# Sliding-window attention and a mixture of experts on one core: attention's loads and stores moved, zeros' products added, the experts' stage in another order

## The chip, the cores and the metric

One NeuronCore of a Trainium2 chip runs the whole program in one launch. The metric is the device time in microseconds of that core; less is better. Its engines are TensorE (matrix products; PE in the profile, PEld its weight loads), VectorE (DVE), ScalarE (ACT), GpSimd (POOL) and SyncE (SP, which here only issues DMAs). Each engine works through its own queue of instructions in the order in which the program has them; they wait for each other by semaphores.

## The reference, cut to what matters

```python
def _attn_ref(q, k, v, n_sink, window):          # q, k, v: 4 x 8 x 768 x 64
    scores = scale * np.matmul(q, k.transpose(0, 1, 3, 2))
    keep = is_sink | in_window                   # 4 sinks, window of 128
    scores = np.where(keep, scores, -1000000000.0)
    a = np.exp(scores - max); a = a / (sum + 1e-09)
    return np.matmul(a, v)

def _moe_ref(x, w_gate, w1, w2):                 # x: 3072 x 512, 8 experts
    logits = x @ w_gate; cap = N // E
    order = np.argsort(-logits.flatten())        # best (token, expert) pairs first,
    ...                                          # an expert takes at most cap = 384 tokens
    for e in range(E):
        h = np.maximum(x[mask] @ w1[e], 0.0)     # 512 -> 1024
        out[mask] = h @ w2[e]                    # 1024 -> 512
```

## The kernel before, in words

**Attention** (`attention`, line 16) works on 24 blocks of 128 queries, numbered c: four batches of six. A block has products of queries and keys (`QK0`, `QK1`), masking and maxima on VectorE (`cp`, `mx`, `nm`), exponentials on ScalarE (`e0` to `e3`), transposes (`T`), copies (`pe0`, `pe1`), GpSimd's masking of the two diagonals (`A`, `B`), products with the values (`AV0`, `AV1`), a product that brings in the sinks (`XS`) and one that turns the result over (`X`), the division by the sums (`xe`) and the logits (`lm`). The block's rows are then stored to `x_dram` in DRAM (`xo`, line 162). Its queries, keys and values are loaded by `ldq`, `ldk` and `ldV` (lines 35 to 37). All of this is one list written out by hand, `SEQ` (line 199): a letter stands for an operation (`KINDS` gives which), and its n-th appearance for the n-th block. Every engine's queue is that list with the other engines' work left out, and so is SP's, which issues the loads and stores. The function `plan` (line 200) hands out buffers in the list's order: five for queries, five for values, six for the rows to be stored. Keys have one buffer a batch. A load has one more dependence, given by `paced` (line 25): it waits for the last activation that stands before it in the list, so that loads are spread over time. A store has none; it waits for its rows.

```python
def paced(d):
    if last: tc.add_manual_dep(d.ins,last[0].ins.name,...,reason="loads spread in time")
```

**The routing** finds for one expert after the other (in an order that the data set) the 384 tokens that it takes. `phase` (line 433) does it in six rounds; each is a compare on VectorE, a count on TensorE (`cnt`, `gather`, line 388), two or four short operations on VectorE, a product that sums over partitions (`dp`, line 483) and a maximum. Then come ranks (`pp`), the tokens' numbers (`ip`, `idx`) and the number of the expert (`ei`). Names are R0 to R7, so R1.dp3 is the sum of the fourth round for the second expert taken.

**An expert** k takes 384 tokens. GpSimd gathers their rows from `x_dram` in three DMAs (`G`, line 572), TensorE turns them over (`X`k.c.t: column block c, gather t; line 580), ScalarE and VectorE split them into a high and a low part (`xh`, `xl`). The weights come in eight chunks of 512 KB (`L`k.j, line 563) through two raw buffers; ScalarE takes the high part (`wh`, line 565), VectorE the low part (`wl`, `W`k.j, line 567), and only then is the raw buffer free for the chunk after the next. `M`k.f.c are the products with the first matrix (line 596; for the first two f of expert 0 lines 593 and 601, where the three products of high and low parts are taken apart), `hh` and `hl` the parts of the hidden values (lines 603 and 604), `N`k.t.f the products with the second (line 612), `y` and `S` the result and its scatter (lines 615 and 617). The order of all this on every engine is made by a list scheduler, `Graph.order` (line 263): it goes by the costs given with each operation, by a table of delays between engines (`ML`, line 238), by a number for each class of operations (`BIAS`, line 647) and by a look-ahead (`WIN`, line 646). The kernel then emits the instructions in that order, engine by engine.

**Zeros' products.** At named places (`FILL`, line 645) `warm` (line 429) puts products on TensorE whose result nobody reads: 128x384 of a matrix of ones, line 431.

Of the kernel before, what the change touches and what calls it, by code (L numbers as in the profile page):

```python
# [9 lines left out]
B,H,S,D=4,8,768,64  # L10
# [158 lines left out]
def layouts(q,k,v,wg,n_sink=4):  # L169
# [24 lines left out]
    P=(3,{'e0 e1 e2 e3':['T','hi','lo','nr']}),nmx=(4,{'nm0 nm1':['e0','e1','e2','e3']}),Z=(4,{'e0 e1 e2 e3':['ra']}),sx=(3,{'hi':['TS']}),  # L194
    PT=(3,{'pe0 pe1':['AV0','AV1']}),pS=(3,{'pS':['XS']}),E=(3,{'A0 A1':['AV0','AV1']}),v=(5,{'ldV':['AV0','AV1','AV0+','AV1+']}),
    r=(4,{'ra':['xe']}),at=(3,{'ae':['X']}),xt=(6,{'xe':['xo','lm']}))
DVEC=()
KINDS={'a': 'QK0', 'b': 'QK1', 'c': 'cp0', 'd': 'mx0', 'e': 'nm0', 'f': 'ldq', 'g': 'e0', 'h': 'fill', 'i': 'cp1', 'j': 'mx1', 'k': 'nm1', 'l': 'e1', 'm': 'e2', 'n': 'e3', 'o': 'U', 'p': 'Uc', 'q': 'um', 'r': 'gs', 's': 'ldk', 't': 'ldV', 'u': 'T', 'v': 'pe0', 'w': 'gl', 'x': 'pe1', 'y': 'nr', 'z': 'hi', 'A': 'A0', 'B': 'A1', 'C': 'lo', 'D': 'TS', 'E': 'pS', 'F': 'B0', 'G': 'AV0', 'H': 'B1', 'I': 'AV1', 'J': 'gc', 'K': 'vh', 'L': 'ae', 'M': 'vr', 'N': 'XS', 'O': 'ra', 'P': 'r', 'Q': 'lds', 'R': 'X', 'S': 'xe', 'T': 'lm', 'U': 'xo', 'V': 'fi', 'W': 'pr0', 'X': 'pr2', 'Y': 'pr1', 'Z': 'pr3', '0': 'pr5', '1': 'pr12', '2': 'pr15', '3': 'pr14', '4': 'pr4', '5': 'pr8', '6': 'pr6', '7': 'pr7', '8': 'pr13', '9': 'pr9', '!': 'pr11', '#': 'pr16', '$': 'pr10'}
SEQ='a b c d e f g h5 b a i j k l c d e m n h4 o p q r s t t i j k u g l h2 a v w m n s f x c d e y l f g b i h1 a j k z z m b n A B h1 u x c C h2 D C d E F h1 G H I y s e i J j k v m K L u l M h2 N g O P Q n R S a c v u B x f D y A E b d e s t O O v x T H P P F g i j B A z l G C I H L a c N F D E k n J t d R S G y s I e O m y L b g l u v a N z i x j k K C f D E z A c m R n O B F G d P e l S H I L g b i u A C D P f j t E a F c k d s B x v t m H G I L N R e n b s u S f g N R i l a s v x t b j k m S n c y d z C O D E B e z C l s P g u v x A i F y O G j M k H B I L A T z n a c H F d D E A U f e y F m N R S G I L b u t f C D g l a E O i T j P v k G x c d e B y N R U H I U t t T T m n S L s B b i l g u x T s z C D A F E y j k v a c d e n H G I a m u z L b g l c y A B f U F O d v N x e C D i E l g f O j k P P P R S s G H I b L t A N F J K B R m z C i n D E j k O S u n m G v U U f T T T H I L a x u x v N R c d b t a z e g S i j P s k l C D E t T c d N f y e n m B A F H G I L R S b A i y j O U u s k g l O U v f x n a N z C D R E m P c P d B F e y l G H I S L b O u U U i t z C s A g v D F E x j y k a z B C n O m c d e H G I b M L i u j y N f R P t l k s g a v x z S m B n b c d e N D f E g U A V F i j k R l C S f G H I s L a c d e b m n D i u z E V B H A F j t P s x B k H v A l G I f a g u t L F n N m v O c x y P R y S f d e N R S C D E b i J T z t l f G z u A B g j V V I s k C a x v O O L P K U N F n D c E P m d e H l t z T B M R S G I t A L b u a g i C v x y H V N j s k m D E n t R c d F G e I A S b g u L y y C D l i B x H a v b j k T T F E c d G B I O O n m e l z i j k T A U z y g U L t u x P C a F v m N D O E T C c T d T V e R G n g S H I l A W X b D F E z C Y Z B u v i 0 1 U G H j t x 2 I k L y U P P N R O 3 n A L B P m N O D T E F P u S v T 4 z y H A R S x 5 C G 6 7 O I D L T F 8 9 E ! # U U U P N N R S G U U $ B H I L U R S U T T N R S T U'
def plan():  # L200
# [38 lines left out]
    'VS':900,'SD':1500,'VD':1700,'PD':1250,'AD':1700,'ED':1250,'DA':900,'DV':900,'DP':900,'DE':1600,'DD':0,'EP':220,'PQ':1560,}  # L239
# [68 lines left out]
class Moe:  # L308
# [336 lines left out]
FILL={'R0.cnt0': 5, 'R0.dp0': 2, 'R0.cnt1a': 6, 'R0.dp1': 2, 'R0.cnt2a': 4, 'R0.dp2': 2, 'R0.cnt3a': 4, 'R0.dp3': 2, 'R0.cnt4a': 4, 'R0.dp4': 2, 'R0.cnt5a': 4, 'R0.dp5': 2, 'R0.pp': 6, 'R0.ipa': 11, 'R1.cnt0': 28, 'X0.0.2': 2, 'X0.0.1': 2}  # L645
WIN=[78.745, 153117.18, 70.288]
# [96 lines left out]
```

## Time and profile before

| what | us |
|---|---|
| median of three runs | 478.67 (474.13 to 479.41) |
| the profiled execution's own time | 476.45 |
| its span, first to last instruction | 474.7 |
| TensorE busy in the span | 444.3 |
| VectorE busy | 368.3 |
| ScalarE busy | 226.4 |
| GpSimd busy | 158.8 |

The profile is one execution, recorded by the chip. A busy TensorE is not TensorE at its peak: ends of products are modelled, and products overlap with the weight loads. "Idle before" names what ended an engine's idle time, inferred from semaphores; "issue" is time in which nothing that the profile shows was waited for. The granted clock is TensorE's, as a share of 2.4 GHz: 1.00 is 2.4, 0.50 is 1.2.

### The profile page before, as it was taken

The numbers are of one execution on the slowest core, as the hardware profiler recorded it, in microseconds if no ns is written. First come the engines' busy times: TensorE is split into PE (matmuls) and PEld (weight loads), VectorE is DVE, ScalarE is ACT, GpSimd is POOL, SyncE is SP. The second block draws the span as 40 slices with busy tenths as digits, with TensorE's granted clock in tenths as the row PEclk, the third lists the DMA queues.
The fourth block names the chain that finished last, engine by engine and source line by source line (L and its number), as shares of the span: only waits on it lengthen the run. The fifth ranks groups of instructions, "written<-read, shape, count | busy, mean of one in ns | idle before, by whom it ended". The sixth has DMA issues, their size and how long they took to land.

```text
span 474.7 us, 14189 instructions
## 1 busy us (share of the span) xinstructions
PE 444.3 (94%) x5526; PEld 367.7 (77%) x5530; DVE 368.3 (78%) x1145; ACT 226.4 (48%) x647; POOL 158.8 (33%) x295
## 2 busy tenths in 40 slices
PE   8798898989978799999999999999999999999994
PEld 4587686777844598778879879878978889988983
DVE  5798798989996889988989988989998975462110
ACT  4987787978700253353344235325435345363111
POOL 5686567778820200410311042041051154002001
PEclk9999999999999999999999999999999999999998
DMA  8645748575520642762554464256255256643001
GB/s 288 205 142 184 228 145 277 176 223 166 175 97 0 204 139 88 219 196 68 161 176 152 138 218 135 89 181 212 97 170 190 99 185 215 210 151 135 23 22 44
DMA packets 44907, 73.86 MB, mean 156 GB/s; under 512 B 3608, under 2 KB 21272, under 8 KB 44840
## 3 DMA queue, kind: packets, MB, share of 16 engines
q1 hardware_dynamic: 40536, 59.78, 39.7%
q0 software_dynamic: 3872, 12.65, 7.6%
q8 instruction: 43, 0.70, 0.6%
q10 hardware_dynamic: 432, 0.52, 0.3%
q14 instruction: 24, 0.20, 0.1%
HBM read 60.34 MB, written 12.60 MB: 154 GB/s over the span
## 4 chain that ended last, share of the span: by engine, by line
PE 60%; DVE 19%; DMA 7%; ACT 6%; issue 6%; POOL 2%; POOLq 0%; DVEq 0%; ACTq 0%; SPq 0%
PE ph L596 21%; PE py L612 18%; DMA raw<-w 5%; PE pp L147 5%; DVE wl L567 4%; PE pp L93 4%; ACT P L24 3%; DVE cmp L363 3%; PE pp L156 2%; PE pr L388 2%; PE pp L128 2%; PE pt L580 2%; ACT PT L24 2%; DMA dum<-ident,row 1%; ACT wh L565 1%
## 5 line engine op out<-in xcount | busy, mean ns | idle before, releaser
L565 ACT ACTIVATE wh<-raw 128x1024 fp32r<-128x1024 f32 x64 | 67.7, 1060 | 81.0 <-DMA raw<-w 53.8
L567 DVE TENSOR_TENSOR wl<-raw,wh 128x1024 fp32r<-128x1024 f32 x64 | 78.1, 1220 | 16.6 <-ACT wh L565 16.3
L596 PE MATMUL ph<-xh,wh 128*128 128x384 f32 x248 | 87.0, 351 | 0.0
L596 PE MATMUL ph<-xh,wl 128*128 128x384 f32 x248 | 83.6, 337 | 0.0
L596 PE MATMUL ph<-xl,wh 128*128 128x384 f32 x248 | 83.4, 336 | 0.0
L612 PE MATMUL py<-wh,hh 128*128 128x512 f32 x192 | 79.4, 413 | 0.0
L572 POOL DMA_INDIRECT xg<-x_dram,idx x24 | 29.8, 1242 | 144.1 <-issue 64.0
L617 POOL DMA_INDIRECT out<-yo,idx x24 | 33.1, 1379 | 129.4 <-ACT yo L615 100.8
L612 PE MATMUL py<-wh,hl 128*128 128x512 f32 x192 | 75.4, 393 | 0.0
L612 PE MATMUL py<-wl,hh 128*128 128x512 f32 x192 | 75.3, 392 | 0.0
L24 ACT ACTIVATE P<-pp,nmx 128x136 f32<-128x136 f32 x192 | 69.4, 389 | 9.5 <-DVE nmx L107 8.1
L603 ACT ACTIVATE hh<-ph 128x384 fp32r<-128x384 f32 x64 | 31.2, 489 | 77.6 <-PE ph L596 71.5
L604 DVE SCALAR_TENSOR_TENSOR hl<-ph,hh 128x384 fp32r<-128x384 f32 x64 | 35.0, 552 | 22.6 <-ACT hh L603 21.0
L596 PEld LDWEIGHTS ph<-xh,wh 128*128 128x128 f32 x248 | 46.8, 189 | 2.6 <-issue 0.4
L596 PEld LDWEIGHTS ph<-xl,wh 128*128 128x128 f32 x248 | 46.7, 188 | 1.9
L596 PEld LDWEIGHTS ph<-xh,wl 128*128 128x128 f32 x248 | 46.6, 188 | 0.0
L93 PE MATMUL pp<-kk,q 64*64 64x204 f32 (+2 forms) x768 | 43.0, 327 | 3.7 <-issue 2.8
L24 ACT ACTIVATION_READ_ACCUMULATOR P<-pp,nmx 128x1 f32 x192 | 42.6, 222 | 0.0
L612 PEld LDWEIGHTS py<-wh,hl 128*128 128x128 f32 x192 | 36.0, 188 | 8.3 <-DVE hl L604 0.2
L135 POOL TENSOR_TENSOR E<-PT,me 128x256 f32<-128x256 f32 x48 | 34.9, 736 | 17.6 <-ACT PT L24 17.6
L612 PEld LDWEIGHTS py<-wh,hh 128*128 128x128 f32 x192 | 36.3, 189 | 4.6 <-issue 0.4
L612 PEld LDWEIGHTS py<-wl,hh 128*128 128x128 f32 x192 | 36.2, 189 | 4.0
(174 smaller groups left out, 785.3 us busy)
## 6 DMA issues: line engine op xcount, KB each, us to landing
raw<-w SPq DMA_DIRECT2D x64, 512.0 KB, 3.9
kk<-kd SPq DMA_DIRECT2D x23, 272.0 KB, 4.5
v<-vd SPq DMA_DIRECT2D x24, 256.0 KB, 3.3
x_dram<-xt SPq DMA_DIRECT2D x24, 256.0 KB, 3.4
q<-qd SPq DMA_DIRECT2D x22, 256.0 KB, 3.7
vx<-vs SPq DMA_DIRECT2D x1, 432.0 KB
xg<-x_dram,idx POOLq DMA_INDIRECT x24
out<-yo,idx POOLq DMA_INDIRECT x24
```

What stands on the lines that cost most here:

```text
L24: def act(*a,**k): last[:]=[nc.scalar.activation(*a,**k)]
L93: PE.matmul(sp[o,s,260*u+a:260*u+204],q[p,2*g+u,o],kk[p,2*i-2+f+a//68:2*i+f+1,2*g+u],start=True,stop=True)
L135: def op_A(c,g): G.tensor_tensor(T('E',c)[:,2*g:2*g+2],diag(c,g),me[:,None].to_broadcast([128,2,2,64]),OP.mult)
L147: PE.matmul(av[half(s),u,a:a+64*n],T('v',c-w)[half(u),256*l+64*x:256*l+64*x+64],m.rearrange("p a n->p (a n)"),start=g==0 and n==2 and w==0 ...
L565: g.add('A',947,lambda wh=wh,raw=raw: nc.scalar.activation(wh,raw,AF.Copy),[f'raw{q}'],[f'wh{s}'],f'H{k}.{j}',f'W{k}')
L567: g.add(e,{'V':1160,'P':2303}[e],lambda wh=wh,wl=wl,raw=raw,e=e: (nc.vector if e=='V' else nc.gpsimd).tensor_tensor(wl,raw,wh.bitcast(F32) ...
L572: g.add('P',1650 if k<4 else 1200,lambda t=t: nc.gpsimd.indirect_dma_start(out=self.xg[t],out_offset=None,in_=self.x_dram,in_offset=bass.I ...
L596: nc.tensor.matmul(p[:,0:CAP],x[:,c,:],y[:,c,:],start=c==0 and i==0,stop=c==3 and i==2)
L603: g.add('A',371,lambda f=f,p=p: nc.scalar.activation(self.hh[:,f,:],p[:,0:CAP],AF.Relu),ps,[f'hh{f}'],f'hh{k}.{f}',f'H{k}')
L604: g.add('V',469,lambda f=f,p=p: nc.vector.scalar_tensor_tensor(self.hl[:,f,:],p[:,0:CAP],0.0,self.hh[:,f,:].bitcast(F32),op0=OP.max,op1=OP ...
L612: nc.tensor.matmul(p,x[:,f,ts],w,start=f==0 and i==0,stop=f==7 and i==2)
L617: st=nc.gpsimd.indirect_dma_start(out=self.out,out_offset=bass.IndirectOffsetOnAxis(ap=idx[:,t:t+1],axis=0),in_=y,in_offset=None)
```

## The change

Four things differ.

1. `SEQ` has the same operations in the same order apart from the loads (`ldq`, `ldk`, `ldV`, and `gs`, `gl`, `lds` for small tables) and the stores (`xo`). Those stand at other places, and partly in another order among themselves. Since `KINDS` is numbered anew, nearly every letter differs; spelled out, the other operations, attention's own zeros' products among them, agree one by one. Before, one load (queries of block 4) stands ahead of the first product; now five do (queries and keys of block 4, values of blocks 1 to 3).
2. `FILL`: 13 instead of 5 zeros' products before R0.cnt0; at expert 0's transposes 4 instead of 2 before X0.0.2, 4 before X0.0.0 (none before), 3 instead of 2 before X0.0.1; 1 before M0.0.0.
3. `ML`, one cost in `rows`, `WIN` and `BIAS`: the scheduler's table. Its result is another order in the experts' stage.
4. The instructions of routing 0 stand in the same order as before.

```diff
-SEQ='a b c d e f g h5 b a i j k l c d e m n h4 o p q r s t t i j k u g l h2 a v w m n s f x c
...
+SEQ='a b c c c d e b f g h i j5 e d k l m n f g h a a o p j4 q r s t u k l m b v i n j2 d w o p
...
-    'VS':900,'SD':1500,'VD':1700,'PD':1250,'AD':1700,'ED':1250,'DA':900,'DV':900,'DP':900,'DE':1600,'DD':0,'EP':220,'PQ':1560,}
+    'VS':900,'SD':1500,'VD':1700,'PD':1250,'AD':1700,'ED':1250,'DA':900,'DV':900,'DP':900,'DE':1000,'DD':0,'EP':220,'PQ':1560,}
...
-            g.add('P',1650 if k<4 else 1200,lambda t=t: nc.gpsimd.indirect_dma_start(
+            g.add('P',1300 if k==0 else 1650 if k<4 else 1200,lambda t=t: nc.gpsimd.indirect_dma_start(
...
-FILL={'R0.cnt0': 5, ... 'R1.cnt0': 28, 'X0.0.2': 2, 'X0.0.1': 2}
+FILL={'R0.cnt0': 13, ... 'R1.cnt0': 28, 'X0.0.2': 4, 'X0.0.0': 4, 'X0.0.1': 3, 'M0.0.0': 1}
-WIN=[78.745, 153117.18, 70.288]
+WIN=[67.356, 243976.036, 690.264]
-BIAS={'G0': 8273289, 'G1': 8166236,
...
+BIAS={'G0': 8739940, 'G1': 8396608,
...
```

Three places show what moved. The first is SP's queue at the end of attention: loads of values (`v`), and stores of the blocks' rows (`x_dram<-xt`; six buffers in turn). Before:

```order
L162 DMA x_dram<-xt_266 128x512
L162 DMA x_dram<-xt_267 128x512
L37 DMA v_178<-vd 128x512
L162 DMA x_dram<-xt_268 128x512
L37 DMA v_177<-vd 128x512
L162 DMA x_dram<-xt_269 128x512
L162 DMA x_dram<-xt_270 128x512
L162 DMA x_dram<-xt_271 128x512
L162 DMA x_dram<-xt_266 128x512
```

After:

```order
L37 DMA v_176<-vd 128x512
L162 DMA x_dram<-xt_268 128x512
L37 DMA v_178<-vd 128x512
L37 DMA v_177<-vd 128x512
L162 DMA x_dram<-xt_269 128x512
L162 DMA x_dram<-xt_270 128x512
L162 DMA x_dram<-xt_271 128x512
L162 DMA x_dram<-xt_266 128x512
L162 DMA x_dram<-xt_267 128x512
```

One store stood between the two last loads of values, and two ahead of them; now the two loads stand together, one store ahead of them, and all others come behind. The loads' places in the list of operations are earlier as well: that of block 23's values moved from behind the maxima of block 23 to behind a small copy (`hi`) of block 21.

The second is TensorE's queue at expert 0's transposes: L580 the transposes of one gather (four column blocks), L483 the product R1.dp0, L431 the zeros' products. Before:

```order
L580 MATMUL py_3258<-idt,xg_3241 128x128
L483 LDWEIGHTS wt_68
L483 MATMUL pr_3251<-i_112,wt_68 128x8
L580 MATMUL pt_3255<-idt,xg_3239 128x128
L580 MATMUL pt_3256<-idt,xg_3239 128x128
L580 MATMUL py_3257<-idt,xg_3239 128x128
L580 MATMUL py_3258<-idt,xg_3239 128x128
L431 LDWEIGHTS onesb
L431 MATMUL ph_3253<-grid,onesb 128x384
```

After, from the same gather's (xg_3239) transposes on; four zeros' products stand ahead of them:

```order
L580 MATMUL pt_3255<-idt,xg_3239 128x128
L580 MATMUL pt_3256<-idt,xg_3239 128x128
L580 MATMUL py_3257<-idt,xg_3239 128x128
L580 MATMUL py_3258<-idt,xg_3239 128x128
L483 LDWEIGHTS wt_68
L483 MATMUL pr_3251<-i_112,wt_68 128x8
L431 LDWEIGHTS onesb
L431 MATMUL ph_3253<-grid,onesb 128x384
```

R1.dp0 stood ahead of the second gather's transposes and stands behind them now, and three zeros' products stand where two did.

The third is VectorE's queue at the first change of expert: `wl_3235` is the low part of expert 1's chunk 3, `xl_3245` the low part of its gathered rows, `odd`, `two` and `i` the short operations of routing 2. Before:

```order
L363 TENSOR_TENSOR cmp_110<-xb_104,grid 128x768
L466 SCALAR_TENSOR_TENSOR y<-x_102,df 128x24
L567 TENSOR_TENSOR wl_3235<-raw_3208,wh_3220 128x1024
L474 TENSOR_SCALAR odd<-pr_3251 64x16
L583 TENSOR_TENSOR xl_3245<-pt_3255,xh_3243 128x384
L475 TENSOR_TENSOR two<-pr_3251,odd 64x16
L583 TENSOR_TENSOR xl_3245<-pt_3256,xh_3243 128x384
L478 TENSOR_SCALAR odd<-two 32x8
L479 SCALAR_TENSOR_TENSOR i_113<-two,odd 32x8
```

After:

```order
L567 TENSOR_TENSOR wl_3234<-raw_3207,wh_3219 128x1024
L474 TENSOR_SCALAR odd<-pr_3251 64x16
L567 TENSOR_TENSOR wl_3235<-raw_3208,wh_3220 128x1024
L475 TENSOR_TENSOR two<-pr_3251,odd 64x16
L478 TENSOR_SCALAR odd<-two 32x8
L479 SCALAR_TENSOR_TENSOR i_113<-two,odd 32x8
L583 TENSOR_TENSOR xl_3245<-pt_3255,xh_3243 128x384
L485 TENSOR_REDUCE P_117<-pr_3251 128x1
L583 TENSOR_TENSOR xl_3245<-pt_3256,xh_3243 128x384
```

The short operations of a round of routing 2 stood between and behind the two `xl`; now they stand ahead of the first. On TensorE the sum that they lead to, R2.dp2, stood behind the first product of expert 1 (M1.0) and stands ahead of the last step of expert 0 (N0.2) and of the transposes X1.2 and X1.3. Expert 1's chunk 0 (`wl_3232`) stood ahead of the large compare of routing 2's first round and stands behind it.

## Rows read from the trace of the kernel before

**Rows 1.** Busy time by stage; a row: stretch, length, engines' busy us (instructions), clock, DMA share, GB/s.

```profile
core 0: us, PE busy (x) PEld busy (x) DVE busy (x) ACT busy (x) POOL busy (x), PEclk, DMA share, GB/s
0.00:137.00 137.00, 122.42 (x3497) 96.42 (x3501) 115.47 (x361) 103.79 (x463) 95.92 (x247) 1.00 0.62 196
137.00:165.00 28.00, 21.94 (x191) 12.69 (x190) 22.17 (x111) 2.00 (x2) 3.22 (x3) 0.93 0.28 90
165.00:464.00 299.00, 295.97 (x1826) 255.71 (x1825) 230.62 (x676) 119.46 (x181) 57.73 (x43) 0.99 0.45 147
```

**Rows 2.** The page: instructions of TensorE, and packets of the queue called instruction.

```profile
PE 444.3 (94%) x5526; PEld 367.7 (77%) x5530; DVE 368.3 (78%) x1145; ACT 226.4 (48%) x647; POOL 158.8 (33%) x295
...
q8 instruction: 43, 0.70, 0.6%
```

**Rows 3.** Waits of 0 to 137 us: engine, line, releaser, us in total, times, longest.

```profile
PE pp L147 <- issue: 3.5, 5, 1.3
PE pp L93 <- issue: 2.8, 2, 1.7
PE pp L156 <- issue: 1.4, 1, 1.4
```

**Rows 4.** Busy time of single blocks in attention.

```profile
37.14:43.05 5.91, 4.49 (x137) 3.52 (x130) 4.82 (x13) 5.24 (x24) 3.94 (x9) 1.00 0.81 238
43.05:47.46 4.41, 4.06 (x126) 3.46 (x127) 3.57 (x13) 2.46 (x15) 2.72 (x6) 1.00 0.49 175
...
61.93:66.30 4.37, 4.16 (x125) 3.42 (x127) 3.99 (x16) 3.85 (x19) 4.29 (x10) 1.00 0.41 128
75.06:80.76 5.70, 4.03 (x130) 3.20 (x128) 4.57 (x18) 4.80 (x22) 5.43 (x14) 1.00 0.88 284
```

**Rows 5.** SP's last issues in attention, in order of time: start, us, line, what.

```profile
124.84 0.33 SPq L37 DMA_DIRECT2D v<-vd  x1
125.26 12.10 SPq L162 DMA_DIRECT2D x_dram<-xt  x9
```

**Rows 6.** Busy time around the two falls of the clock.

```profile
137.30:139.20 1.90, 0.03 (x2) 0.13 (x2) 1.83 (x10) 0.00 (x0) 0.00 (x0) 1.00 0.46 175
140.20:143.90 3.70, 3.70 (x26) 1.79 (x26) 2.81 (x13) 0.00 (x0) 0.00 (x0) 0.57 0.00 0
...
162.00:163.95 1.95, 0.01 (x1) 0.00 (x0) 1.87 (x4) 0.00 (x0) 0.00 (x0) 1.00 0.55 153
163.95:168.20 4.25, 4.25 (x23) 3.43 (x22) 3.39 (x9) 2.12 (x5) 0.00 (x0) 0.60 0.75 241
```

**Rows 7.** TensorE and ScalarE around expert 0's transposes, in order of time.

```profile
155.74 4.71 PE L431 MATMUL ph<-grid,onesb 128*128 128x384 bf16 x28
...
163.95 0.17 PE L483 MATMUL pr<-i,wt 128*128 128x8 bf16 x1 [1.95 <-DVE i L479]
...
167.02 0.52 PE L593 MATMUL ph<-xh,wl 128*128 128x384 f32 x1
...
167.71 1.06 ACT L565 ACTIVATE wh<-raw 128x1024 fp32r<-128x1024 f32 x1 [0.72 <-DMA raw<-w]
```

**Rows 8.** VectorE and TensorE at the first change of expert, in order of time.

```profile
193.93 1.21 DVE L567 TENSOR_TENSOR wl<-raw,wh 128x1024 fp32r<-128x1024 f32 x1
...
195.48 1.54 DVE L363 TENSOR_TENSOR cmp<-xb,grid 128x1536 bf16<-128x1536 bf16 x1
...
201.54 1.23 DVE L567 TENSOR_TENSOR wl<-raw,wh 128x1024 fp32r<-128x1024 f32 x1 [0.30 <-ACT wh L565]
...
205.63 1.22 DVE L567 TENSOR_TENSOR wl<-raw,wh 128x1024 fp32r<-128x1024 f32 x1 [0.66 <-ACT wh L565]
...
207.09 0.56 DVE L583 TENSOR_TENSOR xl<-pt,xh 128x384 fp32r<-128x384 f32 x1
...
207.71 0.55 PE L580 MATMUL pt<-idt,xg 128*128 128x128 f32 x3 [0.85 <-DVE xl L583]
```

**Rows 9.** TensorE's waits for the routing's products, 165 to 464 us.

```profile
PE pr L483 <- DVE i L479: 1.2, 3, 0.7
```

More of the change, by code (lines that the diff above doesn't have):

```diff
@@ L571, in rows @@
         for t in range(3):
-            g.add('P',1650 if k<4 else 1200,lambda t=t: nc.gpsimd.indirect_dma_start(out=self.xg[t],out_offset=None,in_=self.x_dram,in_offset=bass.IndirectOffsetOnAxis(ap=idx[:,t:t+1],axis=0)),
+            g.add('P',1300 if k==0 else 1650 if k<4 else 1200,lambda t=t: nc.gpsimd.indirect_dma_start(out=self.xg[t],out_offset=None,in_=self.x_dram,in_offset=bass.IndirectOffsetOnAxis(ap=idx[:,t:t+1],axis=0)),
                   [f'idx{k}'],[f'xgi{t}',f'xg{t}'],f'G{k}.{t}',f'G{k}')
@@ L644 @@
 LOV=[(k,j) for k in range(E) for j in range(8) if (k,j) not in LOP]
-FILL={'R0.cnt0': 5, 'R0.dp0': 2, 'R0.cnt1a': 6, 'R0.dp1': 2, 'R0.cnt2a': 4, 'R0.dp2': 2, 'R0.cnt3a': 4, 'R0.dp3': 2, 'R0.cnt4a': 4, 'R0.dp4': 2, 'R0.cnt5a': 4, 'R0.dp5': 2, 'R0.pp': 6, 'R0.ipa': 11, 'R1.cnt0': 28, 'X0.0.2': 2, 'X0.0.1': 2}
-WIN=[78.745, 153117.18, 70.288]
-BIAS={'G0': 8273289, 'G1': 8166236, 'G2': 8313964, 'G3': 8285184, 'G4': 8591973, 'G5': 8508460, 'G6': 8002977, 'G7': 8143718, 'H0': 8218728, 'H1': 8486884, 'H2': 8190680, 'H3': 8200275, 'H4': 8381162, 'H5': 7823173, 'H6': 8600931, 'H7': 7822329, 'L0': 8422387, 'L1': 8394305, 'L2': 8333367, 'L3': 8264129, 'L4': 8936856, 'L5': 8269110, 'L6': 8934574, 'L7': 8578857, 'M0': 8284227, 'M1': 8108470, 'M2': 7462474, 'M3': 8219272, 'M4': 8425641, 'M5': 8193347, 'M6': 8476673, 'M7': 8199036, 'R0': 8250122, 'R1': 8987792, 'R2': 8590969, 'R3': 8249864, 'R4': 8442203, 'R5': 8550846, 'R6': 8480417, 'R7': 8195126, 'T0': 8242063, 'T1': 8199801, 'T2': 8327074, 'T3': 8250407, 'T4': 8296951, 'T5': 8187130, 'T6': 8291040, 'W0': 8194866, 'W1': 8275508, 'W2': 8015855, 'W3': 8266282, 'W4': 8009242, 'W5': 8168909, 'W6': 8164546, 'W7': 8293682, 'X0': 8354018, 'X1': 8555277, 'X2': 8283306, 'X3': 8508961, 'X4': 8579196, 'X5': 8423851, 'X6': 8362770, 'X7': 8476510, 'Y0': 8155555, 'Y1': 8477540, 'Y2': 8675100, 'Y3': 8172377, 'Y4': 8989516, 'Y5': 8218612, 'Y6': 8201906, 'Y7': 8171135}
@@ new lines @@
+FILL={'R0.cnt0': 13, 'R0.dp0': 2, 'R0.cnt1a': 6, 'R0.dp1': 2, 'R0.cnt2a': 4, 'R0.dp2': 2, 'R0.cnt3a': 4, 'R0.dp3': 2, 'R0.cnt4a': 4, 'R0.dp4': 2, 'R0.cnt5a': 4, 'R0.dp5': 2, 'R0.pp': 6, 'R0.ipa': 11, 'R1.cnt0': 28, 'X0.0.2': 4, 'X0.0.0': 4, 'X0.0.1': 3, 'M0.0.0': 1}
+WIN=[67.356, 243976.036, 690.264]
+BIAS={'G0': 8739940, 'G1': 8396608, 'G2': 8710834, 'G3': 8443490, 'G4': 8286127, 'G5': 9104186, 'G6': 8371979, 'G7': 8404381, 'H0': 8344076, 'H1': 8247393, 'H2': 8521725, 'H3': 8248235, 'H4': 9162105, 'H5': 9056363, 'H6': 8337451, 'H7': 8746970, 'L0': 8463229, 'L1': 8351005, 'L2': 8747344, 'L3': 9119486, 'L4': 8340475, 'L5': 8273209, 'L6': 8557515, 'L7': 8430912, 'M0': 8596473, 'M1': 8472069, 'M2': 8260395, 'M3': 8479750, 'M4': 8231296, 'M5': 8439373, 'M6': 8427747, 'M7': 8258873, 'R0': 8736425, 'R1': 8862941, 'R2': 8744589, 'R3': 8578010, 'R4': 8748275, 'R5': 8519621, 'R6': 8673807, 'R7': 8438409, 'T0': 8527409, 'T1': 8762731, 'T2': 8435072, 'T3': 8578106, 'T4': 8257148, 'T5': 8398316, 'T6': 8426809, 'W0': 8415186, 'W1': 8440986, 'W2': 8447975, 'W3': 8404779, 'W4': 8225225, 'W5': 8311597, 'W6': 8287215, 'W7': 8230347, 'X0': 8585561, 'X1': 8597661, 'X2': 8475374, 'X3': 8477555, 'X4': 8478255, 'X5': 8404867, 'X6': 8434103, 'X7': 8425082, 'Y0': 8236164, 'Y1': 8680827, 'Y2': 8193282, 'Y3': 8467905, 'Y4': 8283819, 'Y5': 8824334, 'Y6': 8438625, 'Y7': 8305780}
```

4 lines of the change are left out of this document (2 added, 2 removed).

## Prediction

> **What bounds the kernel now.** I read the busy time by stage first [rows 1]. The reader is to see three stages: attention to 137 us, the routing of expert 0 to 165, and the eight experts to 464; behind them come only the last stores. In the experts' stage TensorE is busy 295.97 of 299.00 us, so only 3.03 us are open there and what an order can win is small. Attention has more: 122.42 of 137.00 us, so 14.6 us are open.
>
> Next I asked what ended TensorE's idle time in attention. The largest entries are not an engine: they read "issue", 3.5, 2.8 and 1.4 us in 8 waits, 7.7 us in sum [rows 3]. The windows of rows 4 say what these are. I cut them where such a wait ended (43.05, 47.46, 80.76) and, for the quiet one, at the same spacing: each window holds 252 to 267 matmuls and weight loads. The page has 5526 + 5530 of them and 43 packets of a queue called instruction, 0.70 MB: 257 instructions a packet [rows 2]. So TensorE runs out of code at the edge of a block of some 256 instructions. The windows also show when: a block took 5.91 and 5.70 us where the DMA engines were 0.81 and 0.88 busy, and 4.41 and 4.37 us where they were 0.49 and 0.41 busy [rows 4]. That is the one place where it matters *when* a load of attention runs, for no load was itself waited for long enough to stand among these entries.
>
> Then the clock. It falls twice to 1.2 of 2.4 GHz: after TensorE stood from 137.30 to 139.20 (0.03 us busy), and after it stood 1.95 us from 162.00; the windows behind these have 0.57 and 0.60 [rows 6].
>
> **The change, part by part.**
>
> *Loads and stores of attention.* Nothing is removed or added: the same loads and stores, the same waits, other places in SP's queue. A load goes right behind the last activation that stands before it in the sequence, so its time in the new order can be read off the activations of the old trace. Doing that for all of them I count the stretches in which the DMA queue works without a break for more than 3.5 us, from 25 us on: six before, together some 41 us, nine after, together some 43 us (0.9 us a transfer of 256 KB, an estimate from the 284 GB/s that the fullest window of rows 4 moved). The longest are the stores at the end, 9 us in both; before they begin at 125.26, behind the load of v for block 23, and are issued in one go [rows 5]; after, that load is six us earlier and so are they. In the old trace nearly each long stretch has one wait for code of more than a microsecond. With as much time in long stretches I expect as many waits: **0 us**. Bounds: all 7.7 us go (-7.7), or three more of the size of L93's (two, 2.8 us) come, +4.2 [rows 3]. The cover that hides loads does not get thinner: the least distance from issue to first use rises from 5.5 to 7.4 us by the same reckoning. Five of these loads now stand ahead of the first product, where one did; they come behind what the first blocks need, in the same queue.
>
> The Trainium skill ("Runtime: NRT & Kernel Launch", section Instruction fetch mechanics) says the code memory is refilled in blocks of 256 instructions and that the cost of crossing a block is mostly hidden; rows 3 and 4 agree with the block and not with the hiding. "DMA: Bandwidth & Descriptors", section Queues, rings and completion order, says each DMA engine goes round-robin over its queues by packet; by that a refill would hardly wait for a long stretch, and the places of the loads would make 0 us of difference. Rows 4 speak against it, so I keep both bounds.
>
> *Zeros' products before the second count of expert 0 (R0.cnt0), 5 to 13.* Eight more at 4.71/28 = 0.168 us [rows 7] are 1.35 us in a gap of 1.90 us in which TensorE does nothing [rows 6]; they delay nothing. If the clock then holds, the routing's TensorE steps gain a little, but VectorE sets the pace there: **-0.1 us**, bounds -0.3 to +0.2.
>
> *Zeros' products and order at X0.* Before, the product R1.dp0 stands behind the first four transposes and waits 1.95 us for VectorE [rows 7]; the second four stand behind it. Now four zeros' products and the second four transposes come ahead of it, so TensorE stands some 0.6 us instead of 1.95 and the clock should hold. From 163.95 to 168.20 it was at 0.60 [rows 6]: (1 - 0.60) x 4.25 = 1.7 us; two zeros' products more on the path cost 0.34: 1.4 us earlier at 168.2. It isn't kept. Chunk 2 of expert 0's weights lands when ScalarE takes it at 167.71 for 1.06 us [rows 7]; VectorE's part (1.23 us, as in rows 8) and three short operations follow, so the next count of routing 1 can't begin before about 171.0. The sixteen products, five corrections and one count before it would be done at 169.6. Kept by then: some 0.3 us, and even that meets the next step. I enter **0 us** here, bounds -1.4 to +0.3.
>
> *Order of the experts' stage.* At the first change of expert the old trace shows the step that ends last: VectorE's low part of chunk 0 at 193.93, of chunk 2 at 201.54 (its load may go only when chunk 0's raw buffer is free), of chunk 3 at 205.63 to 206.85, then xl, and TensorE waits 0.85 us until 207.71 [rows 8]. In the new order chunk 0's stands behind the compare of routing 2 (1.54 us, rows 8), and behind chunk 3's come three short operations (some 0.6 us) before xl; on TensorE, R2.dp2, which needs these, stands ahead of the last step of expert 0 and of the transposes X1.2 and X1.3. By my reckoning chunk 3's still ends near 207.1 (its load waits for chunk 1's, whose place is about the same), xl at 208.2, and the first product of expert 1 comes 0.65 us later for the same work done. Against it: in routing 1 three chains now stand ahead of a chunk's low part, so expert 1 is known some 0.5 us sooner. **+0.2 us**, bounds -1.0 and +2.5 (rival below). At the later changes TensorE waits 1.2 us for the routing's products in three waits [rows 9]; other waits of this sort will stand elsewhere: **0 us**, bounds -2 to +2.
>
> *Sum.* 0 - 0.1 + 0 + 0.2 + 0 = +0.1 us on the profiled execution's 476.45 us (span 474.7 and 1.75 around it): 476.5 us. That execution is 2.2 us below the median 478.67 of the runs shown, which reach from 474.13 to 479.41; one per cent, 4.8 us, is about what a measurement of this kernel can tell from no change.
>
> **The rivals.**
>
> 1. *Code arrives in time.* The new stretches may miss the moments at which TensorE asks for code. Five of the eight waits gone at 0.96 us each are -4.8 us: 471.7; all gone, 468.8. For it: rows 4, the block is a microsecond and more longer under load. Against it: more long stretches, not fewer, and as much traffic.
>
> 2. *More waits for code.* Three more of 1.4 us: 480.7. For it: the last stores begin while TensorE is still at full density, so two block edges may fall into their nine us where one did. Against it: single transfers with air between them elsewhere.
>
> 3. *The first change of expert lets the clock fall* (slower). TensorE comes 1.4 us or more early to R2.dp2 and waits there for chunk 3 and the three operations. It decides at a stand of 1.95 us, after which the old trace shows half clock, while after 0.85 us at 207.71 [rows 8] none is seen. Price: again (1 - 0.60) x 4.25 = 1.7 us, and the later start 0.65: 476.5 - 0.2 + 2.35 = 478.7. Against it: half of the early arrival is spent at routing 1.
>
> 4. *The order keeps what it wins.* If 1.4 us at X0 and half a microsecond of routing 1 last to the end and the 1.2 us of rows 9 go: 476.5 - 3.2 = 473.3. Against it: VectorE is busy 230.62 of 299 us [rows 1], and both changes of expert pass through its queue.
>
> **How the numbers follow.** Forecast 0.38; rival 1 0.20; rival 2 0.16; rival 3 0.13; rival 4 0.13. Faster by over 1% (below 471.7) holds most of rival 1 (0.18) and, as cases may add and runs scatter, a little of rival 4 and the forecast (0.07): 0.25. Slower by over 1% (above 481.3) holds half of rival 2 (0.08) and, for the same reason, some of rival 3 and the forecast (0.07): 0.15. The rest, 0.60, is within 1%. The range reaches from the middle of rival 1, 470.0, to just beyond rival 2, 481.5.
>
> **What would show it.** Right: some seven to eight "issue" waits of TensorE before 137 us with 6 to 9 us in sum; granted clock 1.00 from 140 to 144 and from 164 to 168; X1.2 no earlier against attention's end than the 207.71 of rows 8, behind a wait for R2.dp2 or xl. Wrong: an attention stage of 133 us or less, or of 140 or more; a window of 0.6 clock behind 205 us; or expert 1 beginning 1.5 us and more earlier relative to attention's end, and the lead still there at the end.

## The result and the profile after

The changed kernel takes 483.82 us (median of 4, 481.38 to 485.32) against 478.34 for the kernel before (474.13 to 479.41): ratio 1.0143, 95% interval 1.0096 to 1.019. The same kernel measured again gave 1.0135 (1.0091 to 1.018). So it is slower by 1.4%; I had said 476.5 us, no change, and 481.5 at most. The profiled execution took 484.06 us with a span of 482.4, that of before 476.45 with 474.7. Single executions scatter by a per cent either way. The profiled execution of before is 1.9 us below its median and that of after 0.2 us above, so some 2 of the 7.6 us between these two are scatter. Ratios leave out executions over 1.5% slower than the fastest of their kernel (in edge_loads six of twelve, so that its ratio and its median say different things).

Where the 7.7 us of span came from is read off three instructions of TensorE: the first count of expert 0, the first product of expert 0's weights, one part of the last product (the same in both). First the timeline of the kernel before (start, us, engine, line, what, count), then of the one after:

```profile
136.05 0.43 PE L388 MATMUL pr<-oh,cmp 128*128 128x16 bf16 x8
...
165.90 0.69 PE L593 MATMUL ph<-xh,wh 128*128 128x384 f32 x1
...
467.09 0.39 PE L612 MATMUL py<-wh,hh 128*128 128x512 f32 x1
```

```profile
141.98 0.43 PE L388 MATMUL pr<-oh,cmp 128*128 128x16 bf16 x8
...
171.11 0.44 PE L593 MATMUL ph<-xh,wh 128*128 128x384 f32 x1
...
474.70 0.39 PE L612 MATMUL py<-wh,hh 128*128 128x512 f32 x1
```

Attention's end: +5.93 us. From there to the first product 29.85 became 29.13: -0.72. From there to the last product 301.19 became 303.59: +2.40. The tail is the same within 0.1. So attention holds most of the loss, the routing wins, the experts lose. (Within the experts' stretch another 0.76 is won until the fifth count of routing 1: there after is 4.45 us behind.)

The stages of after, to be set beside [rows 1] (same columns):

```profile
0.00:143.00 143.00, 123.47 (x3501) 96.51 (x3502) 116.43 (x361) 104.56 (x463) 96.19 (x247) 1.00 0.60 188
143.00:171.00 28.00, 24.17 (x210) 13.94 (x208) 22.33 (x110) 2.56 (x4) 3.23 (x3) 1.00 0.30 94
171.00:472.00 301.00, 296.10 (x1824) 253.96 (x1824) 230.55 (x676) 120.37 (x181) 58.47 (x43) 1.00 0.44 145
```

Every engine does the same work in attention (TensorE 123.47 us in place of 122.42) in six us more. What stands in them is told by TensorE's waits up to 143 us (for [rows 3]):

```profile
PE pp L147 <- issue: 7.8, 9, 1.9
PE pp L156 <- issue: 3.0, 3, 1.3
...
PE pp L93 <- issue: 1.3, 2, 0.7
...
PE pp L150 <- DVE vr L84: 1.0, 1, 1.0
```

The three "issue" rows are 12.1 us in 14 waits; in the kernel before all "issue" rows of TensorE were 8.3 in 9 (the 7.7 of [rows 3] and one of 0.6). One of them, 0.4 us at 19 us in both, is no wait for code: the last packet of code had ended 7 us before. And there is a wait for vr that was not there. Three blocks of 256 instructions, two with a wait and one without (for [rows 4]):

```profile
39.62:45.27 5.65, 4.36 (x129) 3.51 (x130) 4.02 (x9) 4.29 (x19) 3.36 (x8) 1.00 0.67 207
...
93.44:99.28 5.84, 3.98 (x127) 3.48 (x127) 4.03 (x10) 4.15 (x23) 4.36 (x9) 1.00 0.61 180
...
108.67:112.87 4.20, 4.20 (x128) 3.53 (x128) 3.98 (x14) 3.74 (x17) 2.11 (x6) 1.00 0.58 149
```

The quiet block had 0.58 of the DMA engines, the one with the longest wait 0.61. The load on the DMA engines does not tell them apart, as I had thought; what does is when the loads are issued. SyncE's issues around the edge at 93.44:

```profile
90.51 2.07 SPq L37 DMA_DIRECT2D v<-vd  x3
92.67 0.86 SPq L36 DMA_DIRECT2D kk<-kd  x2
```

Five loads of 256 to 272 KB in the three us ahead of the edge. The stretches behind it:

```profile
95.00:96.90 1.90, 1.90 (x83) 1.63 (x80) 1.80 (x5) 1.04 (x6) 1.82 (x3) 1.00 0.78 273
97.05:98.00 0.95, 0.37 (x14) 0.29 (x6) 0.92 (x4) 0.95 (x7) 0.82 (x2) 1.00 0.09 32
98.00:99.28 1.28, 0.00 (x0) 0.00 (x0) 0.05 (x1) 1.09 (x7) 0.00 (x0) 1.00 0.51 85
```

The loads' bytes run until 96.9 (273 GB/s). Only then, between 97.0 and 98.1, comes the one packet of the queue called instruction (queue, kind: packets, MB, share):

```profile
q8 instruction: 1, 0.02, 5.4%
```

TensorE runs out of code at 97.4 and goes on at 99.28. Setting each packet of q8 beside the waits in this way, I find that in all twelve waits for code of over 0.2 us in attention TensorE went on 1.2 to 1.6 us after its packet's end. For six of the twelve the edge ahead can be read from a wait too: there the packet began 1.9 to 3.6 us behind that edge, each time with loads or stores issued in the two us ahead of it. Behind the edges at 73.80 and 131.47, with the DMA engines idle, it began after 1.38 and 1.15 us. It does not always wait for the last load: behind 99.28 it began after 2.04 us, with the DMA engines full and a load issued 0.16 us ahead of the edge still running:

```profile
99.28:101.32 2.04, 2.04 (x73) 1.82 (x72) 1.32 (x3) 0.28 (x1) 0.00 (x0) 1.00 1.06 358
```

So a fetch comes late behind loads; how many of them it waits for is not settled.

The wait for vr begins much earlier, in SyncE's queue. The kernel before, then after:

```profile
11.63 0.33 SPq L75 DMA_DIRECT2D g_dram<-gm  x1
...
14.01 1.26 SPq L80 DMA_DIRECT2D gx<-g_dram  x2
```

```profile
9.74 1.61 SPq L37 DMA_DIRECT2D v<-vd  x3
11.40 0.47 SPq L36 DMA_DIRECT2D kk<-kd  x1
12.28 1.50 SPq L35 DMA_DIRECT2D q<-qd  x2
13.87 0.38 SPq L75 DMA_DIRECT2D g_dram<-gm  x1
18.76 1.26 SPq L80 DMA_DIRECT2D gx<-g_dram  x2
```

The store of g goes 2.24 us later, behind seven loads more, and its load, which must wait for the store, 4.75 us later: 4.89 us lie between them where 2.38 did. GpSimd, ScalarE and VectorE pass that on to vr, and TensorE waits 1.0 us at 22 us.

In the routing the clock (third number from the right) holds at 1.00, as forecast (for [rows 6]):

```profile
145.10:150.00 4.90, 3.87 (x38) 2.12 (x38) 3.92 (x23) 0.00 (x0) 0.00 (x0) 1.00 0.01 2
...
169.70:174.00 4.30, 4.15 (x34) 3.14 (x33) 3.95 (x12) 2.70 (x5) 0.00 (x0) 1.00 0.73 242
```

At the first change of expert (for [rows 8]) VectorE and GpSimd now stand like this:

```profile
198.99 1.56 DVE L363 TENSOR_TENSOR cmp<-xb,grid 128x1536 bf16<-128x1536 bf16 x1
...
200.70 1.22 DVE L567 TENSOR_TENSOR wl<-raw,wh 128x1024 fp32r<-128x1024 f32 x1
...
202.36 1.21 DVE L567 TENSOR_TENSOR wl<-raw,wh 128x1024 fp32r<-128x1024 f32 x1
```

```profile
198.01 0.94 POOL L572 DMA_INDIRECT xg<-x_dram,idx  x1 [30.78 <-DVE s L401]
199.25 3.49 POOL L572 DMA_INDIRECT xg<-x_dram,idx  x1 [0.30 <-issue]
203.05 1.35 POOL L572 DMA_INDIRECT xg<-x_dram,idx  x1 [0.30 <-issue]
```

and TensorE waits for what they make:

```profile
204.16 0.50 PE L612 MATMUL py<-wh,hl 128*128 128x512 f32 x1 [0.76 <-DVE hl L604]
...
206.34 0.33 PE L580 MATMUL pt<-idt,xg 128*128 128x128 f32 x1 [0.98 <-DMA xg<-x_dram,idx]
```

The second gather holds GpSimd for 3.49 us where the others took 0.94 and 1.35. That is so in after and rest_only alone. In after_again, the same kernel measured once more, it takes 2.12 us, and TensorE waits for hl and for the compare, not for xg:

```profile
202.85 2.12 POOL L572 DMA_INDIRECT xg<-x_dram,idx  x1 [0.30 <-issue]
207.76 0.50 PE L612 MATMUL py<-wh,hl 128*128 128x512 f32 x1 [0.77 <-DVE hl L604]
209.43 0.46 PE L388 MATMUL pr<-oh,cmp 128*128 128x16 bf16 x12 [0.37 <-DVE cmp L363]
```

From the fifth count of routing 1 until 180 products of the experts are done, before takes 24.5 us, after 26.5, rest_only 26.4, after_again 25.9. So 1.3 us are lost with VectorE's order alone, and 0.6 more where the gather is held for long.

### The profile page after: what moved, and what is told of

The parts are those of the page before. It is cut to its first block, busy times and chain, and to the rows that moved or that the text cites. A ratio compares the mean times of both kernels' runs of the same rounds, so it can differ in the third digit from the quotient of the medians.

```text
span 482.4 us, 14218 instructions
## 1 busy us (share of the span) xinstructions
PE 447.3 (93%) x5546; PEld 367.0 (76%) x5546; DVE 369.3 (77%) x1145; ACT 228.2 (47%) x647; POOL 159.8 (33%) x295
## 4 chain that ended last, share of the span: by engine, by line
PE 53%; DVE 23%; DMA 10%; issue 7%; ACT 4%; POOL 1%; POOLq 0%; SPq 0%; ACTq 0%; DVEq 0%
PE py L612 18%; PE ph L596 15%; DMA raw<-w 7%; PE pp L147 5%; DVE wl L567 5%; PE pp L93 4%; DVE cmp L363 3%; PE pp L156 3%; PE pr L388 2%; ACT P L24 2%; PE pp L128 2%; DVE hl L604 2%; PE pt L580 2%; ACT wh L565 1%; DMA dum<-ident,row 1%
## 5 line engine op out<-in xcount | busy, mean ns | idle before, releaser
L572 POOL DMA_INDIRECT xg<-x_dram,idx x24 | 31.4, 1308 | 128.9 <-PE ph L596 31.0
```

Of the source, the lines that this page charges most:

```text
L572: g.add('P',1300 if k==0 else 1650 if k<4 else 1200,lambda t=t: nc.gpsimd.indirect_dma_start(out=self.xg[t],out_offset=None,in_=self.x_dra ...
```

## The experiments

Theory A: the loss is made in attention, by loads issued ahead of a block's edge, which hold up the code of the next block, and by the late g. The rivals: the order of the experts makes it; the loads are just too dense or too late; the waits have nothing to do with the edges.

**The parts (loads_only, rest_only, zeros_only, early_back).**

```diff
 loads_only:  before.py with
+KINDS=, SEQ=        of the changed kernel
 rest_only:   the changed kernel with
+KINDS=, SEQ=        of before.py
 zeros_only:  before.py with
+FILL=               of the changed kernel
 early_back:  the changed kernel with, in SEQ, at their old places:
+ldq.4 gs ldk.4 ldV.1 ldV.2 ldV.3 gl ldk.5 ldq.5 ldq.6 ldk.6 lds
```

> The kernel before with the changed places of attention's loads and stores alone; zeros, stands and experts' order as before. Theory A (the loads' places make the loss: more waits for code, and the vr wait at 22 us): the first count of expert 0 comes 5 to 6 us later than in the kernel before, TensorE's waits for code before 137 us sum to 12 to 15 us, and the time is 483.5 us (ratio 1.011). Rival B (the loads cost nothing, the order of the experts does it): 478.3 us, ratio 1.000.

> The changed kernel with attention's loads and stores back at their old places: zeros' products, stands and experts' order alone. Theory A: 1.5 us won behind R1.dp0, 2.4 us lost at the first change of expert, 0.9 us lost in the last expert but one: 480 us, ratio 1.004. Rival B (the whole loss is here): 484 us, ratio 1.012. Rival C (what is won at X0 stays, the losses come only from attention's end being later): 476.8 us, ratio 0.997.

> The kernel before with the new counts of zeros' products alone; since the experts' order is the old one, R1.dp0 still stands between the transposes. My prediction's step (what is won behind X0 is absorbed before the next count of routing 1): 478.3 us, ratio 1.000. Rival (it is kept): 476.9 us, ratio 0.997. In both TensorE's clock is 1.0 from 140 to 144 us.

> The changed kernel with the loads and stores up to the second load of vx, and v of block 3, back at their old places. If the wait for vr at 22 us comes from the store and load of g behind eight loads: that wait (1.0 us) is gone, the activations from 24 us on come 1.2 to 1.4 us sooner, and the time is 482.4 us (1.009 of the kernel before). If it comes from something else (the cast of vh, the compute order): it stays at 22 us, and the time at 483.8 us.

Measured: loads_only 482.13 us, ratio 1.0078 (1.004 to 1.0117), "issue" waits 10.0 us (12 to 15 expected), the wait for vr 2.2, the first count of expert 0 at 141.72. rest_only 478.85, 1.0023 (0.9992 to 1.0053). zeros_only 479.63, 1.0021 (0.9981 to 1.0062). early_back 482.37, 1.0085 (1.0046 to 1.0125), "issue" 11.3, no wait for vr. So most of the loss comes with the loads alone and rival B falls; the rest costs a quarter of a per cent, which the interval can't tell from nothing. Putting the early loads back takes the wait for vr away, which settles its cause; that the time fell with it (1.0143 to 1.0085) lies within the two intervals.

rest_only's own profile shows what the rest does: first count of expert 0 at 135.49, first product at 164.60 (29.11, as in after), last product at 469.47 (304.87). At the fifth count of routing 1 it is 1.9 us ahead of the kernel before; 26 us later, with 180 products of the experts done in both, it is level with it (205.2 us in both).

**Aimed loads (aim_before, aim_after).** Loads and stores from block 7 on, placed so that by reckoning (1.05 us from issue to first byte, 0.97 us each, one after the other) none is ahead of a fetch for long:

```diff
 aim_before: before.py;  aim_after: the changed kernel, both with
-SEQ=
+SEQ=   (90 loads and stores, the first 14 as before, 76 moved by that rule)
```

> The kernel before with attention's loads and stores (from block 7 on) at places chosen by one rule alone: a load may start only in the 2 us behind the edge of a block of 256 TensorE instructions, so that the fetch of the next block finds no load ahead of it. Zeros and experts' order as before. Theory A (a fetch waits for the loads that were issued before it, and TensorE stands when it comes late): TensorE's waits for code before 137 us fall from 8 to 10 us to 2 to 4 us, the first count of expert 0 comes 5 to 7 us sooner, and the time is 472 us (ratio 0.988). Rival (code comes late for another reason than the loads, or the waits only change their names): waits of 7 us and more, 477 us.

> The same places of loads and stores with the changed zeros, stands and experts' order. Theory A: attention as in the run just above; the changed order costs 1.1 us as it did with the old loads: 473 us (ratio 0.991). Rival (the changed order costs nothing when attention ends early): 472 us or less.

TensorE's waits in aim_before up to 135 us:

```profile
PE pp L93 <- issue: 2.0, 3, 1.0
PE pp L147 <- issue: 1.8, 4, 0.9
PE pp L147 <- DMA v<-vd: 1.5, 1, 1.5
```

"issue" is 4.0 us in sum (2.9 in aim_after) where the kernel before had 8.3: the waits follow the loads, as theory A says. The time does not follow as it should. aim_before 477.35 us, 1.0004 (0.9965 to 1.0043); aim_after 476.40, 0.9977 (0.9943 to 1.0012). The first count of expert 0 came 1.74 us sooner, not 5 to 7: a load of v came too late by my own placing (1.5 us), and the rest of what was won shows up as many small waits for VectorE and ScalarE, which had used TensorE's pauses to catch up. That last is argued from the list of waits, not shown by a run.

**The edges moved, the loads in place (edge_90, edge_144, edge_256).**

```diff
-    for i in range(7): PE.matmul(pp[0][:,0],wz[:,0:128],wz,start=True,stop=True)
+    narrow=[4]*15
+    def zeros(t,n):
+        for _ in range(n):
+            s=narrow.pop() if narrow else 1; w=512//s
+            for j in range(s): PE.matmul(t[:,0,w*j:w*j+w],wz[:,0:128],wz[:,0:w],start=True,stop=True)
+    zeros(pp[0],7)
...
-fill=lambda c: [PE.matmul(pp[c[0]][:,0,:],wz[:,0:128],wz,start=True,stop=True) for _ in range(c[1])])
+fill=lambda c: zeros(pp[c[0]],c[1]))
 edge_144: narrow=[4]*24      edge_256: narrow=[4]*8+[8]*14+[4]*2
```

> The changed kernel with every load and store where the change put it, and 90 TensorE instructions more ahead of 15 us: fifteen of the zeros' products are split into four of a quarter of the width each. Every edge of a block of 256 instructions so comes 90 instructions earlier against the loads. Theory A: reckoned by loads that go one after the other and a fetch that goes behind those issued before the edge, TensorE's waits for code halve, from 12 us to some 6 us, and the time is 479 us although instructions were added (ratio 1.003). Rival (the loads themselves are late or too dense, the edges have no part in it): the waits stay where they are in the sequence, and the time is 484 us or, with the added instructions, 485.

> A control for the run with 90 more instructions: the changed kernel with 144 more, all 24 zeros' products of attention split in four. By the same reckoning the edges now fall on the loads again: TensorE's waits for code sum to 10 to 12 us as in the changed kernel (the reckoning gives 12.7 against 15.1 for the changed one and 7.4 with 90), and the time is that of the changed kernel or up to 1 us more. Rival (splitting the zeros helps by itself, wherever the edges fall): waits of 5 to 6 us and 481.5 us as with 90.

> A second control: the changed kernel with exactly 256 TensorE instructions more ahead of 22 us (zeros' products split in four or eight, the same columns), so that every edge of a block falls where it fell in the changed kernel, a block number later. Theory A (edges against loads): the waits for code sum to 10 to 13 us again, as in the changed kernel, and stand at the same products. Rival (split zeros help by themselves): 5 to 6 us as with 90 and 144. Its time says little: the split products take TensorE some 5 us longer at the start.

The waits of edge_90, then of edge_256 (line numbers are five higher there):

```profile
PE pp L98 <- issue: 3.7, 4, 2.0
PE pp L155 <- DVE vr L89: 2.3, 1, 2.3
...
PE pp L152 <- issue: 0.9, 2, 0.5
```

```profile
PE pp L152 <- issue: 5.1, 9, 1.6
PE pp L161 <- issue: 2.5, 4, 0.9
PE pp L98 <- issue: 1.8, 2, 1.4
```

With 90 instructions more the "issue" waits fall from 12.1 to 5.3 us; the time, 481.58 us, 1.0095 (1.0062 to 1.0128), can't be told from the changed kernel's 1.0135 (1.0091 to 1.018). edge_144 came out against my reckoning: 6.1 us of waits where it gave 12.7:

```profile
PE pp L152 <- issue: 2.9, 5, 1.4
PE pp L161 <- issue: 2.1, 3, 1.3
```

Its time is 479.09 us, 1.0014 (0.9981 to 1.0046), beside 484.83 of the changed kernel measured along with it: 144 instructions more, every load in place, and 1.2% less. That left the rival open that split zeros help by themselves, so edge_256 splits more of them but brings every edge back to its old product: 9.4 us in 15 waits, behind the same lines as in the changed kernel. That is near the 10.0 to 13.1 us of five profiles with these loads and unmoved edges, just below the 10 I had set, and not near 5 to 6. So the edges' places matter for the waits; the reckoning that says by how much is rough. Its one execution took 481.83 us, which leaves open what split zeros do to the time.

**Loads as changed, the rest as before, edges moved (edge_loads).**

```diff
 before.py with SEQ of early_back, and the lines of edge_90
```

> The kernel before, with its zeros and experts' order, and the changed places of attention's loads and stores save the early ones (up to the second load of vx and v of block 3, as before), and the edges 90 instructions earlier. Theory A (the loss that came with the loads is the collision with the edges, and the late g at the start): the waits for code sum to 5 to 7 us, no wait for vr, and the time is 478.5 us (ratio 1.000 to 1.003) though nearly all loads stand where the change put them. Rival (the changed places cost by themselves, by less time between load and use or more conflicts): 481.5 us (1.007).

Measured 481.05 us median of twelve (474.3 to 484.7), ratio 0.9984 (0.9941 to 1.0028); "issue" 8.0 us (5 to 7 expected), first count at 139.64. The median and the ratio say opposite things, so I take it as inconclusive.

**The gather (low_first).**

```diff
+        seq=[i for _,i,_ in sorted(o)]; at={g.t[i][4]:i for i in reversed(seq)}
+        seq.remove(at['W1.0']); seq.insert(seq.index(at['R2.cmp0']),at['W1.0'])
-        for _,i,_ in sorted(o):
+        for i in seq:
```

> The changed kernel with one VectorE instruction moved: the low part of expert 1's chunk 0 stands ahead of the first compare of routing 2, as in the kernel before. Theory (a gather that starts while VectorE is in a long operation waits for its end; that is where 3.5 us of the second gather of expert 1 come from): the second gather takes 1.0 to 1.3 us, the third 1.0 to 1.5, and the first product of expert 1 on gathered rows waits no longer for the gather. Rival (the gather is slow for its rows or its queue): 3.5 us again.

GpSimd's second gather of expert 1 in it, and TensorE's new wait:

```profile
201.15 1.49 POOL L572 DMA_INDIRECT xg<-x_dram,idx  x1 [0.30 <-issue]
```

```profile
203.31 0.46 PE L388 MATMUL pr<-oh,cmp 128*128 128x16 bf16 x12 [0.84 <-DVE cmp L363]
```

The second gather takes 1.49 us in place of 3.49 and TensorE waits no longer for xg. It is a little over my 1.3; VectorE was at the low part (200.60 to 201.82) when it started. But the compare, now later, makes TensorE wait 0.84 us. The stretch behind the fifth count takes 25.8 us, no less than in after_again, and the one execution took 486.46 us: the price moves, it does not go.

**Once more, and a try for a faster version (after_again, aim_stand, aim_stand2).**

```diff
 aim_stand:  before.py, FILL of the changed kernel, aimed SEQ with 4 us and more ahead of each use, and in run():
+        seq.remove(at['R1.dp0']); seq.insert(seq.index(at['X0.3.0'])+1,at['R1.dp0'])
 aim_stand2: in its place
+        for c in range(4):
+            x=at[f'X0.{c}.0']; seq.remove(x); seq.insert(seq.index(at['R1.dp0']),x)
```

> The changed kernel once more, with more rounds, beside the runs of this call. If the parts add (loads alone 1.0078, the rest alone 1.0023): ratio 1.010, 482.8 us. If the two make each other worse, as the first measurement suggests: 1.014, 484.7 us.

> An attempt at a version faster than both: the kernel before with its experts' order, loads and stores behind the edges as in the aimed runs but at least 4 us ahead of their first use (the aimed run lost 1.5 us to one late v), the changed counts of zeros, and R1.dp0 behind the eighth transpose of X0 instead of the fourth. Theory: waits for code 3 us, no wait for v over 0.5 us, expert 0's transposes end 1.5 us sooner than in the aimed run beside attention's end: 474.5 us (ratio 0.993). Rival (what is won in attention and at X0 is taken back by VectorE in the experts): 477.5 us.

> The attempt at a faster version with the step at X0 mended: the four transposes of the second gather stand ahead of R1.dp0, R1.dp0 itself and all VectorE work in their old order; loads aimed, zeros as changed, experts' order of the kernel before. Theory: attention's end 2.5 us and X0's end 3.5 us sooner than in the kernel before, 302.5 us from the first product of expert 0 to the last, as the old order took in five profiles (301.3 to 304.5): 474.5 us, ratio 0.993. Rival (VectorE takes it back): 477.5 us.

after_again: 484.83 us, 1.0135, "issue" 13.1 us, the wait for vr 2.1. The parts add to 1.010; the whole is above that, but the intervals (1.0091 to 1.018 against 1.004 to 1.0117 and 0.9992 to 1.0053) allow both. aim_stand: 477.75, 1.0000 (0.9968 to 1.0032); there R1.dp0 stands behind VectorE's reduce of its product, so the rows of expert 1 are others, while the amount of work is the same. aim_stand2: 477.71, 0.9971 (0.9935 to 1.0006). Both were to be 474.5 us with 3 us of waits for code. Attention is the same in both, instruction by instruction, and the one profile of each has 5.1 us of waits with the first count at 133.93, and 8.0 with it at 139.60: the aimed places don't keep the loads off the edges in every execution. Of all versions this and aim_after (0.9977) are the fastest; neither can be told from the kernel before.

The profiles side by side (us; "issue" waits of TensorE in attention, wait for vr, start of the first count of expert 0, and how often the granted clock stood at half (1.2 of 2.4 GHz), each time for 3.4 us, ahead of that count):

```
loads of before:   before       8.3  -    136.05  0
                   zeros_only   6.7  -    137.44  1
                   rest_only    5.7  -    135.49  0
changed loads:     after       12.1  1.0  141.98  0
                   after_again 13.1  2.1  145.04  1
                   loads_only  10.0  2.2  141.72  1
                   early_back  11.3  -    141.16  0
                   low_first   11.2  1.6  143.55  1
  edges moved:     edge_90      5.3  2.3  139.14  1
                   edge_144     6.1  1.6  139.00  1
                   edge_loads   8.0  -    139.64  1
  moved by 256:    edge_256     9.4  0.3  140.67  1
aimed loads:       aim_before   4.0  -    134.31  0
                   aim_after    2.9  -    134.19  0
                   aim_stand    5.1  -    133.93  0
                   aim_stand2   8.0  -    139.60  2
```

The last column is a cost that I had not looked for. Eight of these ten stretches begin within 0.6 us of the end of a wait of 1.3 to 2.5 us, most of them for code. In zeros_only (clock third from the right):

```profile
55.54:58.05 2.51, 0.01 (x2) 0.01 (x1) 0.63 (x2) 0.64 (x4) 1.71 (x4) 1.00 0.71 231
58.05:61.75 3.70, 3.70 (x48) 2.61 (x52) 1.47 (x5) 1.15 (x4) 0.00 (x0) 0.54 0.03 11
```

So a wait can cost more than its length. Not every long one does: behind the 1.86 us of after that end at 99.28 the clock stays at 1.00. Neither before nor after has such a stretch in attention, so the 5.9 us between them hold none. But two profiles of the changed kernel lie 3.1 us apart at the first count, and a difference of one or two us between single profiles says little.

## Why the prediction was wrong

**The step that failed** is the first term, "with as much time in long stretches I expect as many waits: 0 us". I had the right mechanism (the code of the next block waits for loads) and the wrong measure of it. Not how long the DMA queue works matters, but which loads were issued when TensorE crosses an edge. Both were in my hands: the edges' places are fixed in the program, and I had each load's time in the new order. Whether they would have given the sign, held against each other edge by edge, is not shown: the reckoning of the aimed runs gave 15.1, 7.4 and 12.7 us for after, edge_90 and edge_144, where the profiles have 12.1, 5.3 and 6.1. My upper bound of +4.2 was too low: attention lost 5.9 us in the profile, some 3.8 of it in waits for code and 1.0 in the wait for vr.

**Second failure, in the same paragraph:** of the five early loads I wrote that "they come behind what the first blocks need, in the same queue". I looked at q, k and v and not at the store and load of g, which stand behind them in that queue and feed vr. That is the wait of 1.0 to 2.3 us at 22 us, in six of the seven profiles with the early loads moved (0.3 in edge_256, which starts later) and in none with them at their old places. What is queued behind a moved step, and whom it feeds, was the question to ask of each item.

**Rival 2** had the mechanism, with 0.16, and 480.7 us. It named the last stores as the place; ten of the thirteen longest came between 38 and 103 us, and [rows 5] was the wrong place to look. I had misread it, too: its nine stores are one row because nothing stands between them in the queue. They are issued at 125.26, 125.74, 126.22, 128.03, 128.64, 129.99, 134.19, 135.95 and 137.04 us, not in one go, so there were no nine us of stores on end. My sign for it, an attention stage of 140 us or more, is what came.

**Zeros before R0.cnt0 and at X0:** the clock held, as said: at 1.00 through routing 0 and X0 in all twelve profiles with the new counts, while it falls in three of the four with the old ones. "It isn't kept", 0 us, was wrong: from attention's end to the fifth count of routing 1 after won 1.5 us (5.93 behind, then 4.45), as rest_only did. Some of that is luck of the one profile of before: aim_before, with the old zeros and order, is the fourth, its clock did not fall, and it takes 43.5 us for that stretch, where before takes 44.6 and after 43.1. I took a floor from the old trace: chunk 2 lands when ScalarE takes it, 31.66 us behind the first count [rows 7]. In after ScalarE takes that chunk without waiting for it, 30.22 us behind the first count:

```profile
172.20 1.06 ACT L565 ACTIVATE wh<-raw 128x1024 fp32r<-128x1024 f32 x1
```

So the floor moved by at least 1.4 us. A landing time read from one trace is not a floor for another.

**First change of expert:** +0.2 with a bound of +2.5. After lost 2.0 us there (4.45 behind, then 6.44) and rest_only 1.9, within the bound, but not by chunk 3 and xl, nor by the clock (rival 3: no stretch at half clock stands behind it). It was hl, which stands behind the compare and two low parts on VectorE (1.3 us in after_again, which has no long gather), and in after and rest_only, for 0.6 us more, the gather that met these operations. I had followed xl through VectorE's queue and not hl, and gave the gathers nothing. **Later changes:** 0, and +1.2 measured; the longest single wait there is one of 0.85 us for hl in the last expert but one. Rivals 1 and 4 had nothing to show: no code came sooner, and what the order won at X0 was given back at the next change.

**The sum:** 0 became +5.9, -0.1 and 0 became -1.5, +0.2 became +2.0 and 0 became +1.2: +7.6 on the profiled pair, +5.5 between the medians.

## What to carry to other kernels

Where TensorE's waits read "issue" at a fixed count of instructions, list the edges and the loads issued in the two us ahead of each; here 90 or 144 instructions put in front, with every load in place, halved these waits, and the 144 took 1.2% off the time. When a load is moved forward, go through what stands behind it in its queue by what it feeds, small transfers first. And a pause of TensorE that is taken away is worth its length only if no other engine was using it: 4.3 us fewer waits for code moved attention's end by 1.7, in one profile of each.

## What the hardware showed that I had not expected

Behind the edge at 93.44 the packet of code began after 3.6 us, at 97.05, when the bytes of the five loads of 256 to 272 KB issued before it had all but run out; with the DMA engines idle it began 1.06 us behind an edge in before (133.49), 1.15 and 1.38 in after. The Trainium skill ("DMA: Bandwidth & Descriptors", section Queues, rings and completion order) has each engine go round its queues by packet. By that the packet should have gone in between the loads, and the measurement decides.

GpSimd's indirect DMAs take 0.97 us (median of 23 in after from 150 us on) when they start while VectorE is in none of its operations of over a microsecond, and 1.57 (median of 25, up to 3.49) when they start inside one; in the kernel before it was 0.97 and 1.58, with 24 of each. The third gather of after started at 203.05, in the low part that ended at 203.57, and ended 0.83 us behind that. The Trainium skill ("SBUF — State Buffer", section SBUF: two separate sides) says that GpSimd can't write descriptors while a VectorE operation holds the port that they share; these rows agree. The 3.49 us span two such operations: the gather did not get in between them at 200.55. In after_again it did, and ended 0.83 us behind the compare. What decides that, no run here shows.

Behind a wait for code of 2.5 us the granted clock fell to half in zeros_only (0.54 from 58.05 to 61.75), while behind one of 1.86 us in after it stayed at 1.00.

Left open: why edge_144 is faster than edge_90 (1.0014 against 1.0095) with the same waits in their profiles, and which waits took over in aim_before.
